# A dynamic convolution ahead of an FFN: the conv from the ninth block on in eight 64x32 array tiles instead of four 128x32, issued behind a block's fifth unit instead of its ninth

## The chip, the cores and the metric

One core of a Trainium2 chip runs the kernel. The metric is device time in microseconds (us) from launch to end; the figure for the kernel before is the median of three runs. Profiles show one execution, taken apart by engine: TensorE (PE for matmuls, PEld for weight loads), VectorE (DVE), ScalarE (ACT), GpSimd (POOL) and SyncE (SP, which here only issues DMAs).

## The reference

```python
# x: 8 x 4096 x 192; weight_gen: 8 x 4096 x 8 heads x 7 taps
w = exp(weight_gen - max); w = w / (sum(w) + 1e-9)        # softmax over the 7 taps
x_pad = concatenate([zeros(6 rows), x])                   # per batch
out[b, s, h, :] = sum over k of w[b, s, h, k] * x_pad[b, s + k, 24 values of head h]
h = maximum(out @ moe_w_in, 0)                            # 32768 x 192 -> 32768 x 2048
return (h * h) @ moe_w_out                                # -> 32768 x 192
```

Each token's 192 values are mixed with those of the six tokens before it, with weights of its own per head, and the result goes through a two-layer network with a squared relu between.

## The kernel before, in words

Tokens are taken in 64 subblocks of 512 (`TB`). `BLOCKS` makes 33 blocks j of them: blocks 0 and 1 have one subblock, blocks 2 to 32 have two ("halves" of the block). From j = `FIRST_SPREAD` = 8 on (the ninth block) the conv is `st_conv_spread`, with the first layer's weights in an order of their own (`w_p`). That makes 25 such convs, for blocks 8 to 32, each issued within the block ahead of it, 7 to 31.

**The conv as a matmul.** A piece of 128 tokens of x (`x_t`, 128 partitions, 192 columns, fp16) is the stationary operand, 32 columns at a time. The moving operand is a band matrix `bd`: 128 rows by the piece's output tokens, for each head, with a token's seven weights on the rows of the tokens that it sees. A piece of 128 input rows gives 104 outputs (`STEP`), so a subblock has `NT` = 5 pieces, the last with 96. DVE makes the bands (`st_bands`, `st_band`, L406): it multiplies the softmax rows `wr` (128 tokens by 64 values a piece) with a 0/1 mask, broadcast along the outputs. The rows come from DRAM (`vd`) by `wr_load` on SP's queue, x by `x_load` on POOL's queue; both use `block_load` (L313), one DMA a subblock, or two at a batch's start or where a stored part ends (L317, L321, L327).

`st_conv_spread` (L481) issues 80 matmuls: two rounds of two k, 5 pieces, 2 halves, 2 heads (e). Half and head choose one of four column tiles of the array, 128 rows by 32 columns (`tile_position=(0, p0)`). Each round fills one `yp` of two PSUM banks; ScalarE copies the first to `y`, DVE the second (L512). Then four small DMAs on SP (L516) move the values of heads 6 and 7 to their places in `y`.

**The network.** A unit (`st_unit`) is 128 of the 2048 hidden features for both halves: six matmuls of 64x512 in two row tiles (L581), a relu by ScalarE from PSUM to fp16 (L595), and a square by DVE (L599), for two units at a time but for a block's last two. A block has 16 units, here numbered 0 to 15. The second layer (`st_mm2`, L630) runs one block behind, in quarters-by-halves ("M", 32 matmuls of 64x192 each); with the second half of a quarter come ScalarE's copy and DVE's add of the result (`o_sum`, L644, L646) and, every other time, the store on SP's queue. PSUM: `ps_h` has three two-bank buffers, shared by units and convs; `ps_o` holds one quarter's two banks.

**The order** is written out by hand (`tc.manual_schedule()`): each engine does its instructions in the order in which the loop over `plans[j]` calls them. A plan is a string: "u" a unit, "M" half a quarter, "C" the conv of block j + 1 (and then the x loads of block j + 2), and, put ahead of a unit by `at(j, u, ...)`, "B" the bands of one subblock of block j + 1, "E" an exp of the softmax on ScalarE, "S" a softmax piece on DVE (reduce, reciprocal, products; behind a part's last piece its store to `vd` and the waiting row loads), "L" a load of weights. For blocks 7 to 31 the plan is

```python
steady_spread = "MuMuuu" * 2 + "MuCMuuu" + "MuMuuu"
```

with B ahead of units 1 and 5. Softmax pieces stand ahead of unit 9 in most blocks, ahead of unit 0 in blocks 7 and 10 (`TIMES`). In blocks 12, 16, 20, 24 and 28 the bands are those of a batch whose rows were stored in the block before. At each block's start `load_rows(j + 2)` loads softmax rows, one block ahead of their bands.

## Time and profile before

| what | us |
|---|---|
| runs, median (lowest to highest) | 729.51 (729.48 to 729.95) |
| profiled execution, first to last instruction (span) | 728.4 |
| median less span: what lies around the span | 1.1 |
| PE busy | 722.0 |
| DVE busy | 625.8 |
| ACT busy | 612.0 |
| POOL busy | 98.5 |
| one period, from block 13's conv to block 14's (286.0 to 308.1): PE busy / DVE / ACT | 22.1 / 19.6 / 18.8 |
| all 2000 matmuls of the spread conv | 28.4 |
| all 90 band instructions on DVE | 149.5 |

Busy time of PE and PEld counts overlapping instructions once. A matmul's length in the trace is its latency, since matmuls are pipelined and several tiles work side by side; what it costs the engine is read from the starts. The chain that ended last is followed back from the last instruction, at each step to what released it. A line such as `x32` merges instructions of one kind that follow one another; the number in brackets is the idle time of the engine before it, with what ended it. No execution of the profile's own is timed from outside, so the span is compared with itself and the 1.1 us around it are kept.

### The profile page before, as it was taken

How to read it: one execution, taken by the hardware profiler on the slowest of the kernel's cores; microseconds unless marked ns; L12 is line 12 of the kernel's file. 1: busy time of each engine (PE TensorE's matmuls, PEld its weight loads, DVE VectorE, ACT ScalarE, POOL GpSimd, SP SyncE). 2: the span in 40 equal slices, each digit the busy share in tenths (PEclk: the TensorE clock that was granted, in tenths of full speed). 3: DMA queues.
4: the chain of work that ended last, by engine and by line, in shares of the span. 5: the costliest groups of instructions: out<-in, count | busy, mean ns of one | idle time of the engine just before them, and what ended most of it. 6: DMA issues, size and time to landing. Idle time of an engine off the chain costs nothing.

```text
span 728.4 us, 31046 instructions
## 1 busy us (share of the span) xinstructions
PE 722.0 (99%) x14078; PEld 530.1 (73%) x14078; DVE 625.8 (86%) x839; ACT 612.0 (84%) x731; POOL 98.5 (14%) x146
## 2 busy tenths in 40 slices
PE   8999999999999999999999999999999999999998
PEld 5668877777777777777777777777777777777777
DVE  7999997998898998888988888988888988778753
ACT  6998888888888888888888888888888888888883
POOL 7231223411001100011001010010000110001000
PEclk9999999999999999999999999999999999999999
DMA  9664465676245443356432554343544325444112
GB/s 193 128 113 106 82 125 89 128 142 138 78 71 133 99 84 68 75 116 125 83 62 58 135 104 88 66 74 110 114 78 87 57 53 117 67 87 77 30 46 67
DMA packets 126272, 68.30 MB, mean 94 GB/s; under 512 B 85353, under 2 KB 122556, under 8 KB 125628
## 3 DMA queue, kind: packets, MB, share of 16 engines
q0 software_dynamic: 46192, 19.43, 22.9%
q1 hardware_dynamic: 79804, 46.79, 22.5%
q8 instruction: 110, 1.80, 1.1%
q14 instruction: 22, 0.18, 0.1%
q10 hardware_dynamic: 144, 0.10, 0.0%
HBM read 50.18 MB, written 28.70 MB: 108 GB/s over the span
## 4 chain that ended last, share of the span: by engine, by line
PE 98%; DMA 1%; SPq 0%; ACT 0%; issue 0%; ACTq 0%
PE o L630 47%; PE h L581 44%; PE yp L502 4%; PE h L566 2%; PE yp L536 1%; DMA w_st<-in_moe_w_in_dram 1%; SPq L219 0%; PE yp L466 0%; ACT w_i L740 0%; SPq L135 0%; SPq L133 0%; ACT y L476 0%; SPq L327 0%; SPq L317 0%; ACT o_sb L644 0%
## 5 line engine op out<-in xcount | busy, mean ns | idle before, releaser
L595 ACT ACTIVATE t<-h 128x1024 f16<-128x1024 f32 x512 | 496.6, 1027 | 60.1 <-PE h L581 58.4
L630 PEld LDWEIGHTS <-g 64*128 64x128 f16 (+1 forms) x8032 | 344.3, 94 | 55.2 <-issue 2.3
L630 PE MATMUL o<-w_o,g 64*128 64x192 f16 (+1 forms) x8032 | 380.1, 243 | 0.1
L599 DVE TENSOR_TENSOR g<-t 128x2048 f16<-128x2048 f16 (+1 forms) x287 | 307.4, 1105 | 28.7 <-ACT t L595 28.3
L581 PE MATMUL h<-y,w_p 64*128 64x512 f16 x2400 | 291.7, 376 | 0.0
L581 PEld LDWEIGHTS <-w_p 64*128 64x128 f16 x2400 | 113.9, 94 | 94.8
L406 DVE TENSOR_TENSOR bd<-wr,mask 128x4160 f16<-128x4160 f16 (+4 forms) x90 | 149.5, 1685 | 1.2 <-ACT wr L391 1.2
L646 DVE TENSOR_TENSOR o_sb<-o,o_sb 128x384 f32<-128x384 f32 x123 | 68.4, 556 | 61.4 <-ACT o_sb L644 60.3
L327 POOL DMA_DIRECT2D xt<-in_x_dram x63 | 52.6, 838 | 415.4 <-PE yp L502 362.5
L644 ACT COPY o_sb<-o 128x384 f32<-128x384 f32 x129 | 61.6, 477 | 45.7 <-PE o L630 44.4
L581 PE MATMUL h<-y,w_i 64*128 64x512 f16 x576 | 70.5, 376 | 0.0
L581 PEld LDWEIGHTS <-w_i 64*128 64x128 f16 x576 | 30.5, 94 | 21.7 <-issue 1.2
L502 PEld LDWEIGHTS <-xt 128*32 128x32 f16 x2000 | 24.6, 95 | 10.6 <-issue 10.6
L266 DVE TENSOR_TENSOR v_big<-ex,rcp 128x112 f16<-128x112 f32 (+5 forms) x180 | 29.9, 237 | 2.1 <-DMA vd<-v_big 1.1
L512 DVE CAST y<-yp 128x1024 f16<-128x1024 f32 x25 | 30.4, 1218 | 0.0
L502 PE MATMUL yp<-bd,xt 128*32 128x104 f16 (+1 forms) x2000 | 28.4, 210 | 0.0
L244 ACT ACTIVATE ex<-wg 128x560 f32<-128x560 f32 (+5 forms) x40 | 26.3, 659 | 1.2 <-DMA wg<-in_weight_gen_dram 1.2
L251 DVE TENSOR_REDUCE ssum<-ex 128x80 f32<-128x560 f32 (+5 forms) x40 | 25.6, 639 | 1.3 <-ACT ex L244 1.3
L512 ACT CAST y<-yp 128x1024 f16<-128x1024 f32 x25 | 25.2, 1007 | 0.0
L258 DVE RECIPROCAL rcp<-ssum 128x64 f32<-128x64 f32 (+4 forms) x39 | 23.0, 589 | 1.4
L317 POOL DMA_DIRECT2D xt<-in_x_dram x7 | 3.9, 555 | 120.4 <-PE yp L502 109.4
L361 POOL DMA_DIRECT2D wr<-v_first x24 | 13.0, 559 | 24.0 <-DVE v_first L266 23.8
(42 smaller groups left out, 111.9 us busy)
## 6 DMA issues: line engine op xcount, KB each, us to landing
out_dram<-o_sb SPq DMA_DIRECT2D x63, 384.0 KB
xt<-in_x_dram POOLq DMA_DIRECT2D x42, 240.0 KB, 4.9
wg<-in_weight_gen_dram SPq DMA_DIRECT2D x4, 1064.0 KB
xt<-in_x_dram POOLq DMA_DIRECT2D x21, 192.0 KB, 5.0
wr<-vd SPq DMA_DIRECT2D x38, 80.0 KB
vd<-v_big SPq DMA_DIRECT2D x5, 512.0 KB
y<-y SPq DMA_DIRECT2D x100, 24.0 KB
wg<-in_weight_gen_dram SPq DMA_DIRECT2D x3, 616.0 KB
```

The lines of the kernel that those rows point to most:

```text
L244: nc.scalar.activation(out=self.ex[:, lo:hi].rearrange("p r g k e -> p (r g) k e"), in_=self.wg[:, lo:hi].rearrange("p r (g e) k -> p (r g ...
L266: eng.tensor_tensor(out=bass.AP(tensor=v.tensor, offset=v.offset + lo * H * SL + lo % SL * 2 + g * SL * 2, ap=[list(v.ap[0]), [H * SL + 2, ...
L327: eng.dma_start(out=dst[:, first:last], in_=ap)
L406: nc.vector.tensor_tensor(out=bd_t[j][:, H * lo : H * (lo + len(tiles) * n)].rearrange("p (g m c) -> p g m c", g=shape[1], c=2 * SL), in0= ...
L502: nc.tensor.matmul(out=yp[p0 : p0 + 32, k - k0, a:b], lhsT=x_t[s][:, i, c0 : c0 + 32], rhs=bd[:, head // 2, e, 0 : b - a], start=True, sto ...
L512: copy(out=y[:, k0 : k0 + 2], in_=yp)
L581: nc.tensor.matmul(out=h[:, half], lhsT=w_in_chunk(w, u, slot, half), rhs=y_t[j][r0 : r0 + RT, k], start=(slot == 0), stop=(slot == NK - 1 ...
L595: nc.scalar.activation(out=t1[:, e], in_=h, func=ActF.Relu)
L599: nc.vector.tensor_tensor(out=g[:, a : e + 1], in0=t1[:, a : e + 1], in1=t1[:, a : e + 1], op=AluOp.mult)
L630: nc.tensor.matmul(out=oo[:, cc * Dm : (cc + 1) * Dm], lhsT=g[r0 : r0 + n, cc * P : (cc + 1) * P], rhs=w_o[r0 : r0 + n, fc, :], start=(fc ...
L644: nc.scalar.copy(out=o_sb, in_=o[0][:, c])
L646: nc.vector.tensor_tensor(out=o_sb, in0=o[1][:, c], in1=o_sb, op=AluOp.add)
```

## The change

For blocks from 8 on (subblocks from `FIRST_HALF` = 14), a subblock's 512 outputs are split into two runs of 256 (r = 0, 1), which sit on partitions 0 to 63 and 64 to 127. Each run has `NW` = 5 pieces of 64 input tokens: four of 56 outputs and one of 32 (that last piece starts at 192 of the run's 256 tokens, so that its inputs end with the run). A matmul has 64 rows by 32 columns of the array, and row half, half and head choose one of eight tiles. A conv has 160 matmuls for 80. The two row halves write different banks of `yp` (its shape is now [P, 2 (r), 2 (k), 256]); the copies to `y` put the order back.

The bands of a subblock are 2048 columns for 4160 and are made by two DVE instructions, of 1792 (pieces 1 to 4) and 256 (piece 5), with a mask `mask_half` made on POOL at the start. Loads of x and of softmax rows take four DMAs a subblock (five and a small memset on POOL at a batch's start).

In the plan of blocks 7 to 31 the conv stands behind unit 4 instead of unit 8, and the bands ahead of units 0 and 3 instead of 1 and 5.

```diff
+    HT = TB // 2
+    FIRST_HALF = BLOCKS[FIRST_SPREAD][0]
+    WSTEP = RT - SL
+    windows = [(WSTEP * i, WSTEP * i - SL) for i in range(HT // WSTEP)]
+    windows.append((WSTEP * len(windows), HT - RT))
+    NW = len(windows)
+    w_ends = [a for a, _ in windows[1:]] + [HT]
...
+    mask_half = const.tile([P, RT, 2], f16, name="mask_half")
...
+    def half_load(j, dst, src, width, eng):
+        t0 = (j % NBB) * TB
+        for r in (0, 1):
+            a, p = t0 + HT * r, RT * r
+            first = int(a == 0)
+            if first:
+                nc.gpsimd.memset(dst[0:SL, 0], 0.0)
+                eng.dma_start(out=dst[SL:RT, 0], in_=src[0 : RT - SL, :])
+            eng.dma_start(
+                out=dst[p : p + RT, first : NW - 1],
+                in_=bass.AP(
+                    tensor=src.tensor, offset=src.offset + (a + windows[first][1]) * width,
+                    ap=[[width, RT], [WSTEP * width, NW - 1 - first], [1, width]],
+                ),
+            )
+            b = a + windows[-1][1]
+            eng.dma_start(out=dst[p : p + RT, NW - 1], in_=src[b : b + RT, :])
...
+    def half_bands(j):
+        bd_t[j] = p_bd.tile([P, H * NT * STEP], f16, name="bd")
+        for lo, hi in ((0, NW - 1), (NW - 1, NW)):
+            a, start = windows[lo]
+            n, shift = w_ends[lo] - a, a - start
+            shape = (P, HP * (hi - lo), n // SL, 2 * SL)
+            nc.vector.tensor_tensor(
...
+                in1=mask_half[:, shift : shift + n]
...
-            yp = ps_h.tile([P, 2, TB], f32, name="yp", tag="h")
+            yp = ps_h.tile([P, 2, 2, HT], f32, name="yp", tag="h")
             k0 = min(ks)
             for k in ks:
-                for i in range(NT):
-                    a, b = bounds[i], bounds[i + 1]
+                for (a, _), b, i in zip(windows, w_ends, range(NW)):
                     for half in (0, 1):
...
-                            nc.tensor.matmul(
-                                out=yp[p0 : p0 + 32, k - k0, a:b],
-                                lhsT=x_t[s][:, i, c0 : c0 + 32],
-                                rhs=bd[:, head // 2, e, 0 : b - a],
...
-                                tile_position=(0, p0),
-                            )
+                            for r in (0, 1):
+                                nc.tensor.matmul(
+                                    out=yp[p0 : p0 + 32, r, k - k0, a:b],
+                                    lhsT=x_t[s][RT * r : RT * (r + 1), i, c0 : c0 + 32],
+                                    rhs=bd[RT * r : RT * (r + 1), head // 2, e],
...
+                                    tile_position=(RT * r, p0),
+                                )
...
-        steady_spread = "MuMuuu" * 2 + "MuCMuuu" + "MuMuuu"
+        steady_spread = "MuMuuu" + "MuCMuuu" + "MuMuuu" * 2
...
             if j + 1 >= FIRST_SPREAD:
-                us = (1, 5)
+                us = (0, 3)
```

More of the change, by code (lines that the diff above doesn't have):

```diff
@@ L113, in row_select, with band_mask @@
         )
-    def band_mask():
+    def band_mask(mask, n):
         nc.gpsimd.memset(mask, 1.0)
-        flat = mask.rearrange("p c e -> p (c e)")
-        for sign, base in ((1, 0), (-1, 2 * KK - 1)):
-            nc.gpsimd.affine_select(
-                out=flat, in_=flat, pattern=[[sign, 2 * P]], compare_op=AluOp.is_ge,
-                fill=0.0, base=base, channel_multiplier=-2 * sign,
-            )
+        for p0 in range(0, P, n):
+            flat = mask[p0 : p0 + n].rearrange("p c e -> p (c e)")
+            for sign, base in ((1, 0), (-1, 2 * KK - 1)):
+                nc.gpsimd.affine_select(
+                    out=flat, in_=flat, pattern=[[sign, 2 * n]], compare_op=AluOp.is_ge,
+                    fill=0.0, base=base, channel_multiplier=-2 * sign,
+                )
     x_st = {}
@@ L327, in block_load @@
         eng.dma_start(out=dst[:, first:last], in_=ap)
+    def half_load(j, dst, src, width, eng):
[15 more added lines that the diff above has]
+            eng.dma_start(out=dst[p : p + RT, NW - 1], in_=src[b : b + RT, :])
     def x_load(j):
         x_t[j] = p_x.tile([P, NT, D], f16, name="xt")
+        if j >= FIRST_HALF:
+            return half_load(j, x_t[j], x[j // NBB], D, nc.gpsimd)
         block_load(j, x_t[j], x[j // NBB], D, nc.gpsimd)
@@ L349, in wr_load @@
         wr = wr_t[j].rearrange("p t g c -> p t (g c)")
-        block_load(j, wr, vd_t[j // NBB], H * SL, nc.sync)
+        load = half_load if j >= FIRST_HALF else block_load
+        load(j, wr, vd_t[j // NBB], H * SL, nc.sync)
     def wr_load_sbuf(j, parts, order, engines):
@@ L419, in st_band @@
         )
+    def half_bands(j):
[5 more added lines that the diff above has]
+            nc.vector.tensor_tensor(
+                out=bd_t[j][:, H * a : H * w_ends[hi - 1]].rearrange(
+                    "p (g m c) -> p g m c", g=shape[1], c=2 * SL
+                ),
+                in0=wr_t[j][:, lo:hi]
+                .rearrange("p t g c -> p (t g) c")
+                .unsqueeze(2)
+                .broadcast_to(shape),
+                in1=mask_half[:, shift : shift + n]
+                .rearrange("p (m c) e -> p m (c e)", c=SL)
+                .unsqueeze(1)
+                .broadcast_to(shape),
+                op=AluOp.mult,
+            )
     quads = []
@@ L486, in st_conv_spread @@
         for ks in ((NK, NK - 1), (0, 1)):
-            yp = ps_h.tile([P, 2, TB], f32, name="yp", tag="h")
+            yp = ps_h.tile([P, 2, 2, HT], f32, name="yp", tag="h")
             k0 = min(ks)
             for k in ks:
-                for i in range(NT):
-                    a, b = bounds[i], bounds[i + 1]
+                for (a, _), b, i in zip(windows, w_ends, range(NW)):
                     for half in (0, 1):
                         s = s0 + half
-                        hi = a + (STEP if tile_start(s, i) == starts[i] else b - a)
-                        bd = bd_t[s][:, H * a : H * hi].rearrange(
+                        bd = bd_t[s][:, H * a : H * b].rearrange(
                             "p (g c e) -> p g e c", g=HP, e=2
@@ L501, in st_conv_spread @@
                             c0 = min(G * head, D - 32)
-                            nc.tensor.matmul(
-                                out=yp[p0 : p0 + 32, k - k0, a:b],
-                                lhsT=x_t[s][:, i, c0 : c0 + 32],
-                                rhs=bd[:, head // 2, e, 0 : b - a],
-                                start=True,
-                                stop=True,
-                                skip_group_check=True,
-                                tile_position=(0, p0),
-                            )
+                            for r in (0, 1):
[3 more added lines that the diff above has]
+                                    rhs=bd[RT * r : RT * (r + 1), head // 2, e],
+                                    start=True,
+                                    stop=True,
+                                    skip_group_check=True,
+                                    tile_position=(RT * r, p0),
+                                )
             copy = nc.vector.tensor_copy if k0 == 0 else nc.scalar.copy
-            copy(out=y[:, k0 : k0 + 2], in_=yp)
+            copy(
+                out=y[:, k0 : k0 + 2].rearrange("p k (r c) -> p k r c", r=2),
+                in_=yp.rearrange("p r k c -> p k r c"),
+            )
         for p0 in range(0, P, 32):
@@ L658, in st_bands @@
     def st_bands(j):
+        if j >= FIRST_HALF:
+            return half_bands(j)
         first = int(j % NBB == 0)
@@ L703 @@
         spin(46)
-        band_mask()
+        band_mask(mask, P)
         s0_cuts = (0, FIRST // 2, FIRST, s0.rh)
@@ L751 @@
         nc.gpsimd.memset(v_big, 0.0)
+        band_mask(mask_half, RT)
         steady = "MuMuuu" * 3 + "MuuuMCu"
-        steady_spread = "MuMuuu" * 2 + "MuCMuuu" + "MuMuuu"
+        steady_spread = "MuMuuu" + "MuCMuuu" + "MuMuuu" * 2
         plans = {
```

## The prediction

> **What bounds the kernel now.** I read the page first: busy shares, the chain that ended last, the groups of instructions.

> ```profile
> PE 722.0 (99%) x14078; PEld 530.1 (73%) x14078; DVE 625.8 (86%) x839; ACT 612.0 (84%) x731; POOL 98.5 (14%) x146
> ...
> PE o L630 47%; PE h L581 44%; PE yp L502 4%; PE h L566 2%; PE yp L536 1%; DMA w_st<-in_moe_w_in_dram 1%; SPq L219 0%; PE yp L466 0%; ACT w_i L740 0%; SPq L135 0%; SPq L133 0%; ACT y L476 0%; SPq L327 0%; SPq L317 0%; ACT o_sb L644 0%
> ...
> L406 DVE TENSOR_TENSOR bd<-wr,mask 128x4160 f16<-128x4160 f16 (+4 forms) x90 | 149.5, 1685 | 1.2 <-ACT wr L391 1.2
> ...
> L502 PE MATMUL yp<-bd,xt 128*32 128x104 f16 (+1 forms) x2000 | 28.4, 210 | 0.0
> ```

> The last chain is TensorE nearly throughout, so only time taken from or put into PE's stream counts. The spread conv is 4% of the chain: 25 of them, 28 us. Bands (L406) are the largest DVE item that the change cuts, but DVE is not in the chain. The granted clock is 1.00 in every window after 40 us, so I correct nothing for clock.

> Next the timeline of block 14, around one conv. Columns: start, length (both us), engine, line, operation, how many, and in brackets the idle time before.

> ```profile
> 297.65 0.69 DVE L599 TENSOR_TENSOR g<-t 128x1024 f16<-128x1024 f16 x1
> ...
> 299.14 2.11 PE L581 MATMUL h<-y,w_p 64*128 64x512 f16 x18
> ...
> 299.85 0.56 DVE L646 TENSOR_TENSOR o_sb<-o,o_sb 128x384 f32<-128x384 f32 x1 [1.50 <-ACT o_sb L644]
> 300.00 2.85 ACT L595 ACTIVATE t<-h 128x1024 f16<-128x1024 f32 x3 [0.18 <-PE h L581]
> 300.33 2.31 DVE L406 TENSOR_TENSOR bd<-wr,mask 128x4160 f16<-128x4160 f16 x1
> ...
> 301.09 1.48 PE L630 MATMUL o<-w_o,g 64*128 64x192 f16 x32
> ...
> 302.41 0.81 PE L581 MATMUL h<-y,w_p 64*128 64x512 f16 x6
> ...
> 302.56 2.35 DVE L599 TENSOR_TENSOR g<-t 128x2048 f16<-128x2048 f16 x2
> ...
> 305.56 2.31 DVE L406 TENSOR_TENSOR bd<-wr,mask 128x4160 f16<-128x4160 f16 x1
> ...
> 307.64 0.81 PE L581 MATMUL h<-y,w_p 64*128 64x512 f16 x6
> ...
> 308.38 1.15 PE L502 MATMUL yp<-bd,xt 128*32 128x104 f16 x80
> ...
> 309.46 1.49 PE L630 MATMUL o<-w_o,g 64*128 64x192 f16 x32
> ```

> See three things. PE runs without a gap. Unit 8 (307.64) is followed by the conv 0.74 later, and the next second-layer quarter comes 1.08 after that: of each conv, 0.93 lies from its first to its last matmul start (0.91 to 0.96 over all 25), the rest drains. And the second band (305.56) ended 0.5 us before the conv, with two squares still behind it.

> **Part 1, the matmuls.** 80 become 160, with 56 columns (32 in the last piece) instead of 104 (96), on eight tiles instead of four. Each tile still gets 20. Starts on one tile lie 47 to 48 ns apart at 104 columns and 44 at 96, so it is the columns that set it. No row has a 64x32 tile. The nearest short one is L383, 64 columns on the whole array, 29 ns from start to start, weight load included. A column costs 0.42 ns (on one tile L581 starts 216 ns apart with 512 columns, L630 83 with 192), so eight fewer are 3 ns less; four column tiles add about 2 (104 columns against that slope from L383). So 27 to 28 ns a round, 0.54 us a conv as the **lower end**. The **upper end** is that a matmul costs PE what it does now, 0.93/80 = 11.7 ns: 160 of them, 1.86 us. In between lies the issue of 16 instructions a round: the first twelve of the conv at 308.38 start within 25 ns, some 2 ns each, which gives 32 ns a round. I take 30 ns, 0.60 us, nearest to L383 and to that burst. Alone this would save 0.33 a conv, with 0.03 more from the shorter last matmul: 25 x 0.36 = 9.0 us.

> [...] L502 starts a matmul every 11.7 ns. [...]

> **Part 2, the wait that takes its place.** The conv now follows unit 4, so it wants PE at 302.41 + 0.74 = 303.15 on block 14's clock. Its half 1 reads the band that is now issued ahead of unit 3; in the changed program's DVE order that band stands behind the squares of units 0 and 1. Those wait for ScalarE's relu of unit 1: start 300.00, 1.02 long, end 301.02, DVE 0.03 later (every such wait in the trace: 32 to 34 ns). The square takes 1.22, and DVE's next begins 0.08 before its end: 302.20. Band lengths lie on a line: 832 elements 0.58, 3328 1.88, 4160 2.32, so 0.15 + 0.52 per thousand; 1792 elements 1.08, 256 elements 0.28. The first band piece ends at 303.28, the second at 303.48; PE starts 0.05 after DVE's end (L466 behind its bands). So the conv does its first 4 matmuls, stands until 303.33, does 32 more, stands until 303.53 for piece 5, and has 124 left: 124 x 3.75 ns = 0.465. Last start 304.00, the next quarter at 304.11 (0.11: today's 0.137 less 64 columns). Today's length would put it at 303.15 + 1.08 = 304.23. **Saved: 0.12 a conv, 3.0 us in 25.** The first band (ahead of unit 0) runs 298.35 to 299.65, before the add at 299.85, and costs nothing. Queued behind the late band are the squares of 2 and 3 and the copy of yp, needed by PE only three units later.

> **Part 3, blocks in which DVE is later still.** Blocks 7 and 10 have a softmax piece at unit 0; in the DVE order it stands ahead of both bands now: in block 10 reduce 0.50, reciprocal 0.45, four products 0.72, 1.6 us. Up to 1.0 of lateness is free, since the square waits for the relu anyway (first band and add end 1.0 before it), so the second band slips by some 0.55: **+1.1 us** for both. In blocks 12, 16, 20, 24, 28 the bands need rows of a batch just stored:

> ```profile
> 248.58 0.34 SPq L280 DMA_DIRECT2D vd<-v_big  x1
> 252.11 0.35 SPq L317 DMA_DIRECT2D wr<-vd  x1
> 252.51 0.97 SPq L327 DMA_DIRECT2D wr<-vd  x2
> ```

> The first subblock now takes five loads on SP instead of two, 0.35 to 0.5 each to issue; the packets of the load issued at 252.51 ended near 254.4. So five end some 3.4 after the first issue, at 255.5, while the band could start at 254.2 (in the other four blocks 0.45, 1.0, 1.7, 1.5 late). Again 1.0 is free: 0.3 + 0 + 0 + 0.7 + 0.5 = **+1.5 us**. Bounds: 0 (loads issue faster) and 6 (1 us more each).

> **At nothing:** DVE's 2 x 0.95 us a block less band work, as PE doesn't wait for it elsewhere. POOL: eight x loads a block for two or three, at 0.55 to 0.85 some 5 us, behind the conv, due 22 us later; without that cover a conv would wait for xt. The second mask, some 2 us on POOL near 17 us, ahead of an x load needed at 30. SP: eight band-row loads instead of two or three, a whole block ahead of their use outside the five blocks. ACT: an exp ahead of unit 4's relu delays the copy of yp by 0.1, with 0.6 to spare. The y copies end earlier than now.

> **Sum.** -3.0 + 1.1 + 1.5 = -0.4 us on the profiled span of 728.4, so 728.0; the runs' median is 1.1 above that span, which I keep: 729.1. A measurement here can tell about 0.2% (1.5 us) from no change.

> **Rivals.**
> - *Cheaper rounds and no late rows* (0.20): rounds run at 27 ns and part 3's rows come in time: 25 x 0.165 = 4.1, less 1.1: 726.5.
> - *No band wait* (0.08): the second band ends 0.4 sooner than in my chain; then all of part 1 counts: 729.5 - 9.0, some 721. Against it: the relu, square and band rows hardly vary.
> - *PE cannot take instructions that fast* (0.35), **slower**: bursts of 2 ns were of a filled queue, and the densest 96 instructions in the trace took 0.525 us, 5.5 ns each. Each 0.1 us of conv beyond 0.60 costs 25 x 0.078 = 1.9 (124 of 160 lie behind the wait). At 1.0 us a conv, 736.9; if the two row halves take turns (1.1 us), 738.8; at 1.86, 754. It decides from 0.70 us a conv, 4.4 ns a matmul.
> - *Late blocks later still* (0.05): rows 1 us later in each of the five, 733.5.
> - That the change doesn't do what it says would be the row halves taking turns; it is counted above.

> **How the numbers follow.** The forecast has 0.32 as a case within 0.2% of now; the cases behind 'slower' are spread over 24 us, so its place is the likeliest. Faster is 0.20 + 0.08 = 0.28, slower 0.35 + 0.05 = 0.40. The range 724 to 740 leaves out the second rival and the end of the third beyond 1.1 us, together under 0.2.

> **What would show it.** Right: conv groups with PE idle behind DVE bands, 0.2 and then 0.1; the next quarter about 1.7 us after unit 4's first start (after unit 8's now 1.82); tile starts 27 to 32 ns apart once the bands are there; block period 21.97 for 22.09; blocks 7, 10, 12, 24 and 28 some 0.3 to 0.7 longer than the rest. Wrong: rounds of over 34 ns, no idle time at the band, or PE waiting for xt or y.

## The result: 760.4 us, and the profile after

The changed kernel takes 760.41 us (median of 4 runs, 758.97 to 762.33) against 729.73 for the kernel before on the same chip: a ratio of 1.042, with a 95% interval of 1.040 to 1.044. It is 30.7 us slower. The prediction was 729.1, next to no change, with a range of 724 to 740: it was wrong. The profiled span went from 728.4 to 759.1, also 30.7, so the trace holds the whole loss.

The page of the kernel after, first the busy times, then the chain that ended last, then the groups of the bands (L459) and of the conv (L554):

```profile
PE 742.0 (98%) x16078; PEld 561.7 (74%) x16078; DVE 582.3 (77%) x875; ACT 614.2 (81%) x731; POOL 171.2 (23%) x305
...
PE o L685 40%; PE h L636 37%; PE yp L554 5%; DMA wr<-vd 2%; DMA vd<-v_big 2%; PE h L621 2%; SPq L347 1%; PE yp L591 1%; SPq L355 1%; DMA w_st<-in_moe_w_in_dram 1%; DVE v_big L275 1%; DVE o_sb L701 1%; DMA xt<-in_x_dram 1%; DVE bd L459 1%; DVE rcp L267 0%
...
L459 DVE TENSOR_TENSOR bd<-wr,mask_half 128x1792 f16<-128x1792 f16 x100 | 64.5, 685 | 7.9 <-DMA wr<-vd 7.9
...
L554 PE MATMUL yp<-bd,xt 64*32 64x56 f16 (+1 forms) x4000 | 42.6, 191 | 2.4 <-DMA xt<-in_x_dram 1.5
```

DVE lost 43 us of work (625.8 to 582.3) and nothing got faster for it. PE is busy 20 us more, and the chain, which was PE throughout, now has legs of row loads (`wr`), of the store to `vd` and of SP's issues. Now the timeline of block 14 around the same conv:

```profile
310.74 1.29 DVE L459 TENSOR_TENSOR bd<-wr,mask_half 128x1792 f16<-128x1792 f16 x2
...
310.96 0.81 PE L636 MATMUL h<-y,w_p 64*128 64x512 f16 x6
311.70 1.54 PEld L554 LDWEIGHTS <-xt 64*32 64x32 f16 x160 [0.42 <-issue]
311.70 1.64 PE L554 MATMUL yp<-bd,xt 64*32 64x56 f16 x160
...
313.27 1.49 PE L685 MATMUL o<-w_o,g 64*128 64x192 f16 x32
```

From the conv's start (311.70) to the next quarter (313.27) pass 1.57, for 1.08 before. The single starts within it: four matmuls, then a stop until 311.883, just after the first band piece's end; a burst at some 2 ns an instruction until 312.007; 86 ns of nothing; and from there to the last matmul at 313.15 one instruction every 4.17 ns, weight loads and matmuls alike (one step in between is 30 ns), so 8.33 ns a matmul.

To add the loss up I cut the span at each conv: from the last first-layer matmul ahead of it to the first matmul behind it. Before, a conv is 1.375 by this measure (25 of them 34.4), and each stretch between two convs is 20.717 to 20.719, without any wait. After:

| part | before | after | difference |
|---|---|---|---|
| 25 convs | 34.4 | 50.9 | +16.5 |
| 24 stretches between convs | 497.2 | 509.3 | +12.1 |
| ahead of the first conv and behind the last | 196.82 | 198.86 | +2.04 |

In eighteen of the 25 blocks a conv is now 1.87 to 1.88 long, called an ordinary conv below, and an ordinary stretch is 20.718, as before. So 12.1 of the loss lies between the convs, where PE's own work is unchanged. One such place, PE in block 31:

```profile
707.74 1.64 PE L554 MATMUL yp<-bd,xt 64*32 64x56 f16 x160
709.31 1.49 PE L685 MATMUL o<-w_o,g 64*128 64x192 f16 x32
710.64 0.59 PE L636 MATMUL h<-y,w_p 64*128 64x512 f16 x3
711.94 0.82 PE L636 MATMUL h<-y,w_p 64*128 64x512 f16 x6 [0.71 <-issue]
```

In the first unit behind the conv PE stops after three matmuls for 0.7 us, and the bracket says "issue": nothing that the profile shows was late. Thirteen blocks have such a stop. Against a stretch that has none they are 9.7 us later by it, 8.6 of these between the convs and 1.1 behind the last. Another 3.2 between the convs are waits of the quarter ahead of unit 4, in six blocks, where DVE was late. What can be missing is the program itself. The row of the instruction queue, before and then after:

```profile
q8 instruction: 110, 1.80, 1.1%
```

```profile
q8 instruction: 125, 2.05, 1.2%
```

Last, SP in block 12, whose band rows come from a batch just stored, and the band that waits for them:

```profile
255.37 0.34 SPq L289 DMA_DIRECT2D vd<-v_big  x1
258.05 0.35 SPq L346 DMA_DIRECT2D wr<-vd  x1
258.45 0.65 SPq L347 DMA_DIRECT2D wr<-vd  x1
259.16 0.60 SPq L355 DMA_DIRECT2D wr<-vd  x1
259.80 0.59 SPq L347 DMA_DIRECT2D wr<-vd  x1
260.45 0.60 SPq L355 DMA_DIRECT2D wr<-vd  x1
```

```profile
262.12 1.29 DVE L459 TENSOR_TENSOR bd<-wr,mask_half 128x1792 f16<-128x1792 f16 x2 [1.13 <-DMA wr<-vd]
```

Each load of half the partitions takes SP 0.59 to 0.65 to issue, more than the 0.35 to 0.5 of the prediction; from the first issue to the band it is 4.07.

### The profile page after: what moved, and what is told of

It reads as the page before. It is cut to its first block, busy times and chain, and to the rows that moved or that the text cites. A ratio compares the mean times of both kernels' runs of the same rounds, so it can differ in the third digit from the quotient of the medians.

```text
span 759.1 us, 35512 instructions
## 1 busy us (share of the span) xinstructions
PE 742.0 (98%) x16078; PEld 561.7 (74%) x16078; DVE 582.3 (77%) x875; ACT 614.2 (81%) x731; POOL 171.2 (23%) x305
## 3 DMA queue, kind: packets, MB, share of 16 engines
q0 software_dynamic: 48464, 19.42, 22.9%
q8 instruction: 125, 2.05, 1.2%
## 4 chain that ended last, share of the span: by engine, by line
PE 86%; DMA 6%; DVE 3%; SPq 3%; issue 2%; ACT 1%; POOL 0%; DVEq 0%; ACTq 0%
PE o L685 40%; PE h L636 37%; PE yp L554 5%; DMA wr<-vd 2%; DMA vd<-v_big 2%; PE h L621 2%; SPq L347 1%; PE yp L591 1%; SPq L355 1%; DMA w_st<-in_moe_w_in_dram 1%; DVE v_big L275 1%; DVE o_sb L701 1%; DMA xt<-in_x_dram 1%; DVE bd L459 1%; DVE rcp L267 0%
## 5 line engine op out<-in xcount | busy, mean ns | idle before, releaser
L685 PE MATMUL o<-w_o,g 64*128 64x192 f16 (+1 forms) x8032 | 394.8, 243 | 2.0 <-DVE o_sb L701 1.9
L685 PEld LDWEIGHTS <-g 64*128 64x128 f16 (+1 forms) x8032 | 359.2, 94 | 48.3 <-issue 8.6
L654 DVE TENSOR_TENSOR g<-t 128x2048 f16<-128x2048 f16 (+1 forms) x287 | 312.0, 1106 | 80.7 <-ACT t L650 80.5
L636 PE MATMUL h<-y,w_p 64*128 64x512 f16 x2400 | 308.7, 376 | 6.1 <-issue 5.9
L636 PEld LDWEIGHTS <-w_p 64*128 64x128 f16 x2400 | 132.6, 94 | 96.7 <-issue 11.3
L347 POOL DMA_DIRECT2D xt<-in_x_dram x100 | 66.8, 668 | 341.1 <-PE yp L554 311.5
L459 DVE TENSOR_TENSOR bd<-wr,mask_half 128x1792 f16<-128x1792 f16 x100 | 64.5, 685 | 7.9 <-DMA wr<-vd 7.9
L355 POOL DMA_DIRECT2D xt<-in_x_dram x100 | 58.7, 587 | 0.0
L554 PEld LDWEIGHTS <-xt 64*32 64x32 f16 x4000 | 37.2, 89 | 15.9 <-issue 11.8
L554 PE MATMUL yp<-bd,xt 64*32 64x56 f16 (+1 forms) x4000 | 42.6, 191 | 2.4 <-DMA xt<-in_x_dram 1.5
L564 DVE CAST y<-yp 128x1024 f16<-128x1024 f32 x25 | 30.6, 1224 | 11.7 <-PE yp L554 11.7
L437 DVE TENSOR_TENSOR bd<-wr,mask 128x3328 f16<-128x3328 f16 (+5 forms) x26 | 33.1, 1310 | 0.9 <-ACT wr L422 0.7
```

The costliest lines, as they stand in the source:

```text
L347: eng.dma_start(out=dst[p : p + RT, first : NW - 1], in_=bass.AP(tensor=src.tensor, offset=src.offset + (a + windows[first][1]) * width, a ...
L355: eng.dma_start(out=dst[p : p + RT, NW - 1], in_=src[b : b + RT, :])
L459: nc.vector.tensor_tensor(out=bd_t[j][:, H * a : H * w_ends[hi - 1]].rearrange("p (g m c) -> p g m c", g=shape[1], c=2 * SL), in0=wr_t[j][ ...
L554: nc.tensor.matmul(out=yp[p0 : p0 + 32, r, k - k0, a:b], lhsT=x_t[s][RT * r : RT * (r + 1), i, c0 : c0 + 32], rhs=bd[RT * r : RT * (r + 1) ...
L564: copy(out=y[:, k0 : k0 + 2].rearrange("p k (r c) -> p k r c", r=2), in_=yp.rearrange("p r k c -> p k r c"),)
L636: nc.tensor.matmul(out=h[:, half], lhsT=w_in_chunk(w, u, slot, half), rhs=y_t[j][r0 : r0 + RT, k], start=(slot == 0), stop=(slot == NK - 1 ...
```

## The experiments

My theory after these views: four causes add up. (1) 320 instructions a conv, at the 4.17 ns each of block 14, take 1.3 us; (2) the late band; (3) waits for pieces of the program, where 256 instructions are used up too fast; (4) rows and x that come too late in the blocks at a batch's start. The rivals: that the array halves take turns or the matmul's size still sets the pace (against 1), and that the waits named "issue" are a semaphore that the profile doesn't name (against 3). The kernel before took 729.87 beside the first four kernels below and 729.88 beside the last four.

**tiles_only**: the eight tiles at the old place.

```diff
-        steady_spread = "MuMuuu" + "MuCMuuu" + "MuMuuu" * 2
+        steady_spread = "MuMuuu" * 2 + "MuCMuuu" + "MuMuuu"
...
-                us = (0, 3)
+                us = (1, 5)
```

> The changed kernel with the conv back behind unit 8 and the bands back ahead of units 1 and 5: the array tiles, half bands and loads alone. Issue theory: TensorE takes one instruction per 4.17 ns once its 64 queued ones are gone, so 160 weight loads and matmuls cost 1.30 to 1.33 us from first to last matmul start against 0.93 before, +0.34 a conv, 25 x 0.34 = 8.5 us; no wait for bands, rows or x. Fetch theory on top: waits at a 256-instruction boundary of up to 0.8 us in the earlier of the 25 blocks, some 5 us. Together 738 to 744 us. Rival, that the tiles themselves are to blame for all: 755 to 760.

Measured: 755.10 (754.72 to 755.58), ratio 1.034 (1.033 to 1.036). That is not the 738 to 744 of the issue and fetch theories but the number of the rival, so this run alone doesn't part them; tiles_phase below does. The stretches between convs sum to 497.2, as before the change: no late row or band costs anything there. All of the loss lies in the convs, 59.6 for 34.4. PE at the first of them:

```profile
153.61 1.18 PE L554 MATMUL yp<-bd,xt 64*32 64x56 f16 x122
155.46 0.44 PE L554 MATMUL yp<-bd,xt 64*32 64x56 f16 x38 [0.67 <-issue]
155.84 1.33 PE L685 MATMUL o<-w_o,g 64*128 64x192 f16 x28
```

The stop is inside the conv, after 122 matmuls. In the last blocks it stands at about the 108th, as a border of the program does that slips a little from block to block. The conv of block 21 has no such wait and takes 1.729. So 25 x (1.73 - 1.375) = 8.9 us is the issue. The other 16.4 are waits, 0.2 to 1.4 us in each of the other convs, most of them at this place: three times the 5 us that I had put down for the program (some 2 of the 16.4 are something else, see tiles_phase).

**move_only**: the old four-tile conv at the new place.

```diff
-        steady_spread = "MuMuuu" * 2 + "MuCMuuu" + "MuMuuu"
+        steady_spread = "MuMuuu" + "MuCMuuu" + "MuMuuu" * 2
...
-                us = (1, 5)
+                us = (0, 3)
```

> The kernel before with the conv behind unit 4 and the bands ahead of units 0 and 3, with the old tiles and the long bands. Band-wait theory, by the chain of the prediction with bands of 2.32 us: second band ends at 304.5 on block 14's clock, conv wanted at 303.15, so 1.4 us of wait a conv: 25 x 1.4 = 35 us, with late blocks 764 to 770 us. Rival, that the move costs only the late rows and the late x of block 7: 732 to 736 us.

Measured: 767.49 (766.78 to 769.34), ratio 1.052 (1.050 to 1.053). Its waits of PE (total, times, longest):

```profile
PE yp L502 <- DVE bd L406: 25.5, 25, 1.2
```

With the old band of 2.32 us the conv waits about 1.0 each time by this row; by its starts it is 1.3 longer each time, 67.2 us for 34.4 in all. As expected: the move by itself loses more than the tiles by themselves, and the shorter bands are what makes it bearable.

**phase_less** and **phase_more**: the changed kernel with fewer or more matmuls in the idle warm-up at the start, which no output uses. They shift every border of the program against the code, by 64 instructions one way and 70 the other, and change nothing else in the program.

```diff
-        WARM = 156
+        WARM = 512
...
-        spin(46)
+        spin(14)
```

```diff
-        WARM = 156
+        WARM = 88
...
-        spin(46)
+        spin(81)
```

> The changed kernel with 14 warm-up matmuls of 512 columns at the start for 46 of 156: the same columns, 64 instructions fewer ahead of everything else. Fetch theory: TensorE's program comes in pieces of 256 instructions, of which a changed block has exactly four; a piece is asked for when the one before it begins and is there some 3.8 us later. The boundary that fell 135 to 163 instructions into the conv now falls 64 later, so the next one is reached 3.8 us or more after it: the waits of 0.3 to 1.2 us three units behind the conv go, 8 us in all: 752 us. Rival, that these waits come from something at a fixed place in the block (the y copies, ScalarE, a store): the same gaps, 760 us.

> The changed kernel with 81 warm-up matmuls of 88 columns at the start for 46 of 156: 70 instructions more ahead of everything else. Fetch theory: the boundary falls 65 to 93 instructions into every conv, and the next one at or just behind its end, some 1.5 to 2.1 us later, while the piece takes 3.8: a wait of 1.7 to 2.4 us in each of the 25 blocks in place of the present 8 us in all: 790 to 810 us. Rival, something at a fixed place in the block: 760 us.

Measured: 761.63 (760.48 to 762.59) and 817.18 (813.87 to 820.02); ratios 1.044 (1.042 to 1.045) and 1.119 (1.116 to 1.123). With 35 more warm-up matmuls at the start the kernel is 57 us slower. In the trace of phase_more, around one conv:

```profile
304.99 1.64 PE L554 MATMUL yp<-bd,xt 64*32 64x56 f16 x160
306.56 0.66 PE L685 MATMUL o<-w_o,g 64*128 64x192 f16 x11
308.90 1.06 PE L685 MATMUL o<-w_o,g 64*128 64x192 f16 x21 [1.68 <-issue]
```

Here the border has moved to just behind the conv. The quarter stops after 11 of its 32 matmuls and goes on 1.9 us late. Its row in the waits of PE (total, times, longest):

```profile
PE o L685 <- issue: 47.0, 26, 3.7
```

That is one wait for each conv and one more. The total is above the expected 790 to 810; behind eight of these stops the granted clock was 0.50 as well (see the last section). A semaphore that the profile doesn't name could not move with the warm-up; the stops moved with the number of instructions ahead of them, as the third cause has it. In phase_less the waits in the units are gone, as expected, and an ordinary conv takes 1.876, an ordinary stretch 20.718. Yet the total did not fall to 752. For one thing, PE now stopped inside twelve of the convs, behind the 113th matmul in block 9 and the 100th in block 30, where the shifted border falls by the expectation's count; the convs are 0.05 to 1.4 us longer by it, some 4.5 in all. Its row in the waits of PE, which leaves out the shorter ones:

```profile
PE yp L554 <- issue: 3.4, 6, 1.3
```

For another, x came later in block 7 (the conv waited 3.0 us for it, for 1.5 in the changed kernel), and the blocks with late rows had become later. SP in block 12 of phase_less:

```profile
256.55 0.34 SPq L289 DMA_DIRECT2D vd<-v_big  x1
...
261.55 0.35 SPq L346 DMA_DIRECT2D wr<-vd  x1
```

Five us from the store's issue to the first load that may follow it, and 3.3 to 4.4 in the other four batches; in the changed kernel 2.6 to 2.8 in all five, before the change 2.9 to 4.1. Nothing in the edit touches that store. What sets its length is left open.

**phase_mid**: a shift of 30 instead of 64.

```diff
-        WARM = 156
+        WARM = 231
...
-        spin(46)
+        spin(31)
```

> The changed kernel with 31 warm-up matmuls of 231 columns for 46 of 156: 30 instructions fewer ahead, the boundary 165 to 193 instructions into the conv. Fetch theory: neither the waits three units behind the conv nor any inside it; what stays is issue (8.9 us), band wait (0.15 a conv, 3.7 us) and late rows and x (7 to 12 us, by the luck of the store): 750 to 754 us. Rival, no fetch waits in the changed kernel: 760 us.

Measured: 752.73 (750.62 to 753.53), ratio 1.031 (1.029 to 1.033). Of the stops in the stretches one of 0.3 us is left, in block 8; block 31's counterpart of the lines above runs through:

```profile
701.56 1.64 PE L554 MATMUL yp<-bd,xt 64*32 64x56 f16 x160
703.13 1.49 PE L685 MATMUL o<-w_o,g 64*128 64x192 f16 x32
704.46 1.89 PE L636 MATMUL h<-y,w_p 64*128 64x512 f16 x16
```

So with the borders moved the kernel is 760.4 - 752.7 = 7.7 us faster. What is left, 22.9, is issue (8.9), the band in every conv (1.877 for 1.730: 25 x 0.147 = 3.7), and 10.3 for the blocks in which rows or x are late. The stops themselves were worth more than 7.7, since late rows and x cost phase_mid some 2 more than the changed kernel: there the 30.7 are issue 8.9, band 3.7, program some 10, rows and x some 8.

**tiles_phase**: tiles_only with such a shift (46 instructions).

```diff
-        WARM = 156
+        WARM = 104
...
-        spin(46)
+        spin(69)
```

> The array tiles alone (conv behind unit 8, bands ahead of units 1 and 5), with 69 warm-up matmuls of 104 columns for 46 of 156: 46 instructions more ahead, so that the 256-instruction boundary falls 169 to 197 instructions into the conv instead of 215 to 243. Issue plus fetch theory: the waits of 0.2 to 1.4 us inside each conv go, 16.4 us in all, and what stays is the issue of 320 instructions, 1.73 us from unit to next quarter against 1.38: 25 x 0.35 = 8.9 us above before, 738 to 740 us. Rival, that the waits inside the conv belong to the conv (its weights, PSUM, the band's second part): 755 us again.

Measured: 741.99 (741.50 to 742.28), ratio 1.017 (1.015 to 1.018). The conv issued in block 10, one of 19 like it among the 25:

```profile
221.89 1.49 PE L554 MATMUL yp<-bd,xt 64*32 64x56 f16 x160
223.31 1.49 PE L685 MATMUL o<-w_o,g 64*128 64x192 f16 x32
```

No wait of any kind, and still 1.42 from its start to the next quarter, for 1.08 with four tiles: the issue alone, without band, program or rows, is +0.355 a conv. The other six convs, in blocks 7, 12, 16, 20, 24 and 28, are 0.24 to 0.44 longer, 2.0 in all, which puts the total 2 us above the range expected. In block 7 a stop of 0.4 at a border is part of it. The rest are stops of 0.07 to 0.21 us at no fixed matmul, not where a new band piece begins. These six are the only convs beside which SP issues DMAs, and each such stop begins 0.07 to 0.26 us after an issue began. Why PE stops there is not shown. Beside phase_mid this run says what the move costs once the tiles are paid for: 752.7 - 742.0 = 10.7 us.

**wide**: the changed kernel with matmuls of up to 104 columns in place of 56.

```diff
+                            wide = b - a if i == NW - 1 else min(STEP, HT - a)
...
-                                    out=yp[p0 : p0 + 32, r, k - k0, a:b],
+                                    out=yp[p0 : p0 + 32, r, k - k0, a : a + wide],
...
-                                    rhs=bd[RT * r : RT * (r + 1), head // 2, e],
+                                    rhs=bd_t[s][RT * r : RT * (r + 1), H * a + e : H * a + e + 2 * wide : 2],
```

> The changed kernel with each matmul of the conv up to 104 columns wide (104, 104, 104, 88, 32 instead of 56, 56, 56, 56, 32), overlapping ones overwritten by the next; it reads the band of the first two heads for all, so that part of the computation is changed. Instructions are the same in number and order. Issue theory: a tile has 66 ns a round from issue and needs 47 for 104 columns, so the conv keeps its 1.87 us: 758 to 763 us. Rival, that the columns or the row halves taking turns set the conv's time: 1.69 times the columns, 0.9 us more a conv, 25 x 0.9 = 22 us more: 780 us or above.

Measured: 759.57, ratio 1.041 (1.039 to 1.043); an ordinary conv 1.892 for 1.875. Its group:

```profile
L555 PE MATMUL yp<-bd,xt 64*32 64x104 f16 (+2 forms) x4000 | 43.0, 206 | 2.2 <-DMA xt<-in_x_dram 1.1
```

Up to 48 columns more a matmul cost 0.017 us a conv: neither columns nor row halves taking turns set the pace of eight tiles here; what stayed the same is the number of instructions and their 4.17 ns each. The first set of rivals falls. No run has the matmuls without as many weight loads, so that the weight loads alone set the 8.33 ns a pair is not excluded.

**two_queues**: phase_mid, with the loads of the second half (r = 1) on POOL's queue.

```diff
             a, p = t0 + HT * r, RT * r
+            eng = nc.gpsimd if r else eng
```

> As the run with the boundary 165 to 193 instructions into the conv, but the loads of the second row half (x and softmax rows) are issued from POOL's queue, so SP issues half as many row loads. Late-row theory: in blocks 12, 16, 20, 24 and 28 the nine row loads of 0.6 us each on SP set when the bands can start; five and four on two queues save 2 us or so a block, in the five blocks some 4 to 8 us unless the store itself is later: 744 to 750 us. Rival, that the wait is for the store alone: the same time as that run.

Measured: 747.75 (747.57 to 751.45), ratio 1.026 (1.023 to 1.028). Five us under phase_mid. The convs of the five batch blocks are 0.4 us longer than ordinary ones in all, for 3.8 in phase_mid (2.2 waits for the band, the rest stops beside SP's issues), so most of the late rows' cost was SP's issue of one load after the other. The execution of 751.45 is the profiled one: in block 28 POOL began its row loads 2.6 us after SP did, and the stretch there is 3.5 longer, part of it at a granted clock of 0.50 (last section). The late x of block 7 stays.

No version beats the kernel before: all have the 160 matmuls or the late band.

## Why the prediction was wrong, point by point

- **What bounds the kernel**: right, and enough to rule out a gain from less DVE work. 43 us less of it gave nothing.
- **Part 1, the matmuls**: this is the step that failed: "I take 30 ns, 0.60 us", said of a round and of a conv. A round, of eight matmuls and eight weight loads, took 66 ns and the conv's starts 1.31 to 1.33 (first to last, without waits). The 2 ns of the burst held for some 64 instructions, then each took 4.17. The row L383, 29 ns a start, says nothing on this: two instructions in 29 ns are no rate of issue. The row that did bear on it was named only in the rival: 96 instructions in 0.525, 5.5 ns each, about the pace of the old conv itself, 160 instructions in 0.93, where 4.17 each would be 0.67. Part 1's 9.0 us gain was an 8.9 us loss.
- **Part 2, the band**: right in mechanism and size. The first band piece stood where it was put and the conv stopped at its fifth matmul for 0.17 to 0.18 in 18 blocks (predicted 0.18). The second wait, predicted 0.1, falls on the 86 ns that stand behind the first 64 instructions anyway (91 ns in tiles_phase, where the band is not late), so all of it costs 0.147 a conv.
- **Part 3, late blocks**: right in the blocks, wrong in size: 2.6 predicted, some 8 in the changed kernel and 10 in phase_mid measured. The softmax pieces cost what was said or less (0.55 each predicted at the conv; it was the quarter ahead of unit 4 that waited, 0.63 in block 10, whose conv was then 0.1 shorter, and 0.32 in block 7). Three other terms were off. The row loads took 0.59 to 0.65 each to issue. The lateness did not end at the conv: DVE's add of the output was late too, and the quarter ahead of unit 4 waited 0.2 to 1.3 in five blocks. And block 7, in which the conv's x was late by 1.5:

```profile
149.39 0.26 PE L554 MATMUL yp<-bd,xt 64*32 64x56 f16 x5
151.12 1.54 PE L554 MATMUL yp<-bd,xt 64*32 64x56 f16 x155 [1.46 <-DMA xt<-in_x_dram]
```

  "Due 22 us later", said of POOL's x loads at nothing, was wrong just there: the conv ahead of it is that of block 7, in the earlier plan, and started only 9.8 us before it, while the eight loads of 0.56 to 0.68 ran on POOL from 141.5 to 147.5. That a conv would wait for xt without that cover had been said, the place not. The other entries at nothing held between the convs: in tiles_phase the stretches there sum to 497.25, for 497.23 before. SP's row loads did not quite cost nothing: beside them stand the stops in six convs of that run.
- **Not in the prediction at all**: the waits for pieces of the program: 7.7 us between the changed kernel and phase_mid, 13.1 between tiles_only and tiles_phase. Each edit that packs instructions closer should have been asked for this.
- **Rivals**: "PE cannot take instructions that fast" (0.35) was the right one. By its own formula 1.31 us a conv would be 729.1 + (1.31 - 0.60) x 25 x 124/160 = 742.9. Issue and band alone make 729.7 + 8.9 + 3.7 = 742.3. The rest, 18 us, is late rows and program.
- **What would show it**: "rounds of over 34 ns" and "PE waiting for xt" were named as signs of a wrong prediction, and both came.

## What to carry to other kernels

When matmuls get smaller and more, count instructions, weight loads too, and take the rate from the densest long stretch of the trace (here 4.17 ns each), not from the spacing of single matmuls nor from a burst (here some 64 instructions at 2 ns each). Where PE started the 320 instructions of a conv within 1.31 to 1.33 us, it stopped in or behind them for up to 3.7 us: put down to "issue", at nearly the same instruction in each iteration, and moved when the number of idle instructions at the start was changed. The kernel's time then hung on where the borders fell: 752.7 to 817.2 us for the same code. Before work is moved earlier, look for the one iteration in which its cover is short (a batch's start, the first of a new plan), and count each DMA's issue by the shape that it will have (here 0.59 to 0.65 us on SP for 0.35 to 0.5 assumed).

## What the runs showed of the hardware that was not expected

- With 56 columns a matmul, in the ordinary convs of the kernel after, TensorE started some 64 instructions in 123 to 126 ns behind the late band, stood for 84 to 89 (91 in tiles_phase), then started one every 4.17 ns; in the run wide that last pace was the same with up to 104 columns. Why the burst ends there is not shown.
- Its program came in pieces of 16 KB (125 packets, 2.05 MB, 32156 instructions). It stopped for up to 3.7 us (phase_more). Counted back 256 instructions from the restart, the border before it lay 3.5 to 3.9 us earlier in twelve of the thirteen stops of the kernel after (3.5 in block 31), 5.0 in block 8, and 3.2 to 3.7 in 22 of the 25 stops of phase_more (an estimate, since the profile marks no border); the 3.8 us of the expectations lies among these. In the twelve a packet of that queue began 0.8 to 1.4 us behind that border and PE went on 1.3 to 1.6 after the packet's end; in the 22 it began 0.8 to 1.3 behind. These times fit a piece being asked for when the one before it begins, but no row shows the asking. The same code took 752.7, 760.4, 761.6 and 817.2 us with the borders at four positions.
- In phase_more the granted clock was 0.981 on average, for 1.00 in the kernel after: it was 0.50 for 3.4 us behind seven of the stops and for 6.8 us behind one, in block 8, and the units that follow the conv there were 0.9 to 2.3 us longer, 11.7 in all. Of the 64 us over phase_mid, 47 are the waits of the row shown. The same 3.4 us at 0.50 stand in phase_less behind stops of 3.1 and 2.4 us (from start to start) in blocks 7 and 12, and in two_queues behind one of 2.5 in block 28; other stops of 2.3 us in phase_more left the clock at 1.00.
- The time from a store's issue to the first load that waits for it ran from 2.6 to 5.0 us between kernels that don't differ in that store.
